# Second layer of a two-layer MoE: single-bank PSUM tiles, another emission order, some differences on GpSimd, two sums moved to the second phase

## The chip, the cores and the metric

The kernel runs on one core of one Trainium2 chip. The metric is device time in microseconds of one execution, as the median of several runs. The profile is of one more execution, and its times are counted from the start of that execution's span.

## The reference

Retention over 4 x 8 heads of 576 x 64 gives a matrix of 2304 tokens x 512. Two feed-forward layers follow, both with w_in of 512 x 2048 and w_out of 2048 x 512, all in float32:

```python
def _moe_ref(x, w_in, w_out):
    h = x @ w_in
    g = h * (1.0 / (1.0 + np.exp(-h)))
    return (g @ w_out).astype(np.float32)

def _moe2_ref(x, w_in, w_out):
    h = x @ w_in
    r = np.maximum(h, 0.0)
    g = r * r
    return (g @ w_out).astype(np.float32)

x = _moe_ref(x, moe_w_in, moe_w_out)
return _moe2_ref(x, moe2_w_in, moe2_w_out)
```

## The kernel before

Every float32 operand of a matmul is split in two: a high part, which ScalarE makes with a cast (L649), and a low part, the difference of value and high part, which VectorE makes (L650). A product of two operands takes three matmuls: high by high, high by low, low by high. `split` issues the cast at once and hangs the difference into `later`, a list that `flush` empties once per step.

Retention and the first layer fill the span up to 477 us. The second layer, which the change touches, is written by hand in two phases. Both use a scheme with seven products of half-size operands in place of eight (as Strassen's, in the form with few sums): operands 0 to 6 on each side are quarters of a matrix or sums of them, called a11, a12, a21, a22 and s1 (a21 + a22), s2 (s1 - a11), s3 (a11 - a21), s4 (a12 - s2). The weights' seven operands lie in DRAM ready made. Product i takes weight class RF[i], with RF = (0, 3, 1, 4, 2, 5, 6).

**Phase one** (`product1`, L719) makes h: three blocks b of tokens, four pairs d of weight columns p = 2d and 2d + 1 in each, and 14 steps k in a pair, k // 2 being the product i and k % 2 the column. A product is six matmuls of 128x384; there are 168 of them. `after1` reads the results from PSUM: a copy s1 by ScalarE after product 0 (L727), sums u2 and u3 of bank and copy by VectorE after products 1 and 3 (L731), then a quarter of h, c, after product 2 (ScalarE, relu, L735) and products 4, 5 and 6 (VectorE, L737). `gate1` turns c into g with relu and square on ScalarE (L748, L749); when the odd column's g is there, the tile is stored to gD in DRAM. S1 and S3 of g are made here, by two VectorE operations per pair (L756), and stored beside the quarters a11, a12 and a22: five tiles a pair.

**Phase two** (`product2`, L811) makes the output: nine sets P of 128 rows of each half, seven products of 24 matmuls of 128x256 in each. `after2` reads them in the same way (L819, L824, L826, L829) and issues the output's DMAs from ScalarE's queue. For set P, five tiles of g are loaded with SP's queue (`load_g`), two sums are made (`sum_g`) and seven operands split (`split_g`); the w2 classes are loaded (`load_w2`, L700, SP) and split (`split_w2`) in the last block of phase one (table in `beside1`) and in set 0 (the lists at the end). g's split for product n stands five products ahead.

One chain is the products 0 to 6 of one column or set. It has two PSUM banks; product i writes bank i % 2, and products 2, 3, 5 and 6 add to what is there. Which tile the chain gets is decided in `chain(n)`: every fourth one gets a single tile "pab" of two banks, the others two tiles of one bank each, "pa" and "pb". The dependencies are kept by tile.

What sets the order is the program's text: each engine's queue runs in the order of emission. In a step of phase one the product comes first, then `beside1` (loads, sums and splits of what comes later), then `flush`, then `after1`. The pool wp has 32 slots for weights, operands on load and g of set 0.

## Time and profile before

| | us |
|---|---|
| three runs | 874.85, 877.52, 878.30 |
| median | 877.52 |
| the profiled execution | 882.85 |
| its span in the trace | 881.0 |

| engine | busy us | share of the span |
|---|---|---|
| TensorE | 834.9 | 95% |
| VectorE | 511.9 | 58% |
| ScalarE | 452.5 | 51% |
| GpSimd | 103.0 | 12% |

The rows that the argument rests on stand in a section of their own below. PE is TensorE, DVE VectorE, ACT ScalarE, POOL GpSimd; SPq and ACTq are the DMAs that SP and ScalarE issue. A row of the timeline gives start, length, engine, line, operation, output<-input, and in brackets how long the engine had been idle before and what released it. GpSimd is idle after 477 us in this kernel.

### The profile page before, as it was taken

How to read it: one execution, taken by the hardware profiler on the slowest of the kernel's cores; microseconds unless marked ns; L12 is line 12 of the kernel's file. 1: busy time of each engine (PE TensorE's matmuls, PEld its weight loads, DVE VectorE, ACT ScalarE, POOL GpSimd, SP SyncE). 2: the span in 40 equal slices, each digit the busy share in tenths (PEclk: the TensorE clock that was granted, in tenths of full speed). 3: DMA queues.
4: the chain of work that ended last, by engine and by line, in shares of the span. 5: the costliest groups of instructions: out<-in, count | busy, mean ns of one | idle time of the engine just before them, and what ended most of it. 6: DMA issues, size and time to landing. Idle time of an engine off the chain costs nothing.

```text
span 881.0 us, 16063 instructions
## 1 busy us (share of the span) xinstructions
PE 834.9 (95%) x6458; PEld 769.1 (87%) x6458; DVE 511.9 (58%) x773; ACT 452.5 (51%) x874; POOL 103.0 (12%) x134
## 2 busy tenths in 40 slices
PE   6899989999999999999999998998997799989997
PEld 5778879999999888888887997998996799989996
DVE  4799984543544344423474777466567676655660
ACT  5687773453545334324464775565676443424430
POOL 3202001322232132201130000000000000000000
PEclk8999999999999999999999998998998999999999
DMA  9565642734546245217625654363597754444200
GB/s 347 176 182 192 216 145 73 227 138 141 172 139 203 108 139 164 89 42 230 200 78 209 215 197 139 108 214 108 193 320 242 282 192 168 157 132 156 97 25 25
DMA packets 70010, 144.96 MB, mean 165 GB/s; under 512 B 5552, under 2 KB 41392, under 8 KB 69936
## 3 DMA queue, kind: packets, MB, share of 16 engines
q1 hardware_dynamic: 63888, 132.66, 45.2%
q10 hardware_dynamic: 6048, 11.27, 3.4%
q8 instruction: 50, 0.82, 0.4%
q14 instruction: 24, 0.20, 0.1%
HBM read 96.21 MB, written 47.71 MB: 163 GB/s over the span
## 4 chain that ended last, share of the span: by engine, by line
PE 71%; ACT 5%; DVE 5%; DMA 4%; issue 2%; ACTq 0%; SPq 0%; DVEq 0%
PE acc L81 18%; PE ph L81 18%; PE pa L811 8%; PE pab L811 6%; PE pb L811 6%; PE pa L719 4%; PE pab L719 4%; PE pb L719 3%; PE Q L390 2%; DMA w2r<-w2c 2%; DMA gD<-g 1%; ACT xa L649 1%; ACT g L749 1%; PE P L339 1%; DMA gr<-gD 1%
## 5 line engine op out<-in xcount | busy, mean ns | idle before, releaser
L604 DVE TENSOR_TENSOR gl<-sg,gh 128x512 fp32r<-128x512 f32 (+1 forms) x80 | 54.6, 682 | 123.8 <-ACT gh L603 123.7
L81 PE MATMUL ph<-xh,wh 128*128 128x512 f32 (+2 forms) x328 | 121.1, 369 | 1.8 <-ACT xh L420 1.8
L601 ACT ACTIVATE sg<-ph 128x512 f32<-128x512 f32 (+1 forms) x80 | 44.2, 552 | 152.6 <-PE ph L81 151.5
L81 PE MATMUL acc<-gh,wh 128*128 128x512 f32 (+1 forms) x320 | 120.0, 375 | 0.0
L81 PE MATMUL ph<-xl,wh 128*128 128x512 f32 (+2 forms) x328 | 119.7, 365 | 0.3 <-DVE xl L422 0.3
L81 PE MATMUL ph<-xh,wl 128*128 128x512 f32 (+2 forms) x328 | 119.6, 365 | 0.0
L81 PE MATMUL acc<-gh,wl 128*128 128x512 f32 (+1 forms) x320 | 118.1, 369 | 0.0
L81 PE MATMUL acc<-gl,wh 128*128 128x512 f32 (+1 forms) x320 | 118.1, 369 | 0.0
L649 ACT CAST gl<-gr 128x1024 fp32r<-128x1024 f32 (+1 forms) x66 | 66.0, 1009 | 82.5 <-DVE y L829 34.8
L650 DVE TENSOR_TENSOR gl<-gr,gl 128x1024 fp32r<-128x1024 f32 (+1 forms) x66 | 77.0, 1174 | 49.9 <-ACT gl L649 49.9
L811 PE MATMUL pab<-w2s,gl 128*128 128x256 f32 x504 | 68.7, 295 | 17.0 <-ACT s L819 6.6
L811 PEld LDWEIGHTS pab<-w2s,gl 128*128 128x128 f32 x504 | 64.9, 201 | 20.6 <-ACT s L819 7.2
L719 PE MATMUL pa<-xa,w1s 128*128 128x384 f32 x432 | 81.9, 335 | 0.3 <-DVE c L737 0.3
L719 PEld LDWEIGHTS pa<-xa,w1s 128*128 128x128 f32 x432 | 75.4, 188 | 0.7 <-DVE c L737 0.6
L811 PE MATMUL pa<-w2s,gl 128*128 128x256 f32 x576 | 72.4, 283 | 0.0
L81 PEld LDWEIGHTS ph<-xh,wh 128*128 128x128 f32 x328 | 61.8, 188 | 10.2 <-ACT xh L420 2.3
L811 PEld LDWEIGHTS pa<-w2s,gl 128*128 128x128 f32 x576 | 70.6, 192 | 0.0
L81 PEld LDWEIGHTS ph<-xl,wh 128*128 128x128 f32 x328 | 61.8, 189 | 7.6 <-DVE xl L422 0.5
L81 PEld LDWEIGHTS ph<-xh,wl 128*128 128x128 f32 x328 | 61.7, 188 | 7.2
L81 PEld LDWEIGHTS acc<-gh,wh 128*128 128x128 f32 x320 | 60.4, 189 | 8.6
L81 PEld LDWEIGHTS acc<-gh,wl 128*128 128x128 f32 x320 | 60.4, 189 | 7.7
L81 PEld LDWEIGHTS acc<-gl,wh 128*128 128x128 f32 x320 | 60.5, 189 | 7.4
(112 smaller groups left out, 1353.9 us busy)
## 6 DMA issues: line engine op xcount, KB each, us to landing
wr<-w SPq DMA_DIRECT2D x64, 512.0 KB, 3.7
gD<-g SPq DMA_DIRECT2D x60, 384.0 KB, 2.9
gr<-gD SPq DMA_DIRECT2D x45, 512.0 KB, 5.1
raw<-att SPq DMA_DIRECT2D x32, 512.0 KB, 4.4
w2r<-w2c SPq DMA_DIRECT2D x14, 512.0 KB, 5.8
xq<-x SPq DMA_DIRECT2D x12, 384.0 KB, 5.4
out<-y ACTq DMA_DIRECT2D x18, 256.0 KB, 2.5
w1c<-wt SPq DMA_DIRECT2D x8, 512.0 KB, 7.9
```

Source lines behind the costliest of these rows:

```text
L81: mm(o, a, b, start=first and i == 0, stop=last and i == n - 1)
L339: mm(o, dims(u, a, e, b, 768), dims(u, a, e, b, 0), start=True, stop=True)
L390: mm(w, a, b, start=e not in started, stop=last)
L601: nc.scalar.activation(s, ph, ACTF.Silu)
L604: later.append(lambda: nc.vector.tensor_sub(gl, s, gh))
L649: nc.scalar.copy(dst[0], src)
L650: later.append(lambda: nc.vector.tensor_sub(dst[1], src, dst[0]))
L719: mm(o, lhs, rhs, start=m == 0 and i in (0, 1, 4), stop=m == 5, skip_group_check=True)
L749: later.append(lambda: nc.scalar.activation(g[:, :, p % 2], c.rearrange("p (t n) -> p t n", t=TT), ACTF.Square))
L811: mm(o, lhs, rhs, start=first, stop=m == NP - 1 and q == 2, skip_group_check=True)
```

## The change

- The PSUM tiles of the second layer come from one pool "pc" of eight tiles of one bank. Every chain takes two of them, in both phases; "pab" is gone. The first layer's PSUM pools are closed before.
- In both phases the reads of product n - 1 are emitted right behind product n and ahead of the loads, sums and splits of step n.
- i = 6 of the gate: one VectorE operation (scalar_tensor_tensor, max with 0, then times c) in place of relu and square on ScalarE.
- S1 and S3 of g are no longer made in phase one; four quarters are stored (48 stores instead of 60), four loaded per set (36 loads instead of 45), and S1 and S3 are made in phase two on VectorE as two more parts of `sum_g`, of 128x1024.
- The low part is made on GpSimd in 38 places: the x operands of blocks 1 and 2 other than operands 0 and 2 (ten of 128x768), the classes with odd c of the w1 columns from the third on (six of 128x512, six of 128x256), all those w2 splits that are called from `beside1` (classes 0, 3, 1 and two quarters of 4, 14 of 128x512), and operand 1 of set 0 (two of 128x512).
- In the last block the loads and splits of w2 and of set 0's g stand at other steps. In phase two the w2 splits start with the third quarter of class 4, and each set's loads and sums have other steps. The pool gq has 6 buffers instead of 7; the pools hl, rq and tq are opened in another order.

The core of the diff:

```diff
...
-    def chain(n):
-        if n % 4 == 0:
-            t = ps_a.tile([128, 2, 512], F32, tag="a", name="pab")
-            return t[:, 0], t[:, 1]
-        pool, tag = (ps_g, "g") if n % 4 == 1 else (ps_o, "o")
-        return tuple(pool.tile([128, 512], F32, tag=tag, name=nm) for nm in ("pa", "pb"))
-
-    def split(dst, src):
+    def chain():
+        return tuple(pools["pc"].tile([128, 512], F32, tag="c", name=nm) for nm in ("pa", "pb"))
+
+    def split(dst, src, engine=nc.vector):
...
-        later.append(lambda: nc.vector.tensor_sub(dst[1], src, dst[0]))
+        later.append(lambda: engine.tensor_sub(dst[1], src, dst[0]))
...
     def split_x(b, i, pool, tag):
...
-        split((t[:, 0], t[:, 1]), x_s[b][i])
+        split((t[:, 0], t[:, 1]), x_s[b][i], nc.gpsimd if b and i not in (0, 2) else nc.vector)
...
-    def split_w2(c, q):
+    def split_w2(c, q, engine=nc.vector):
...
-        split((t[:, 0], t[:, 1]), w2_raw[c, q // 2][:, q % 2 * 512 : q % 2 * 512 + 512])
+        split((t[:, 0], t[:, 1]), w2_raw[c, q // 2][:, q % 2 * 512 : q % 2 * 512 + 512], engine)
...
     def product1(p, b, i):
...
-            sp[p % 2] = {"o": chain(b * NP + p)}
+            sp[p % 2] = {"o": chain()}
...
-        if i != 2:
-            nc.scalar.activation(c, c, ACTF.Relu)
-        later.append(lambda: nc.scalar.activation(g[:, :, p % 2], c.rearrange("p (t n) -> p t n", t=TT), ACTF.Square))
+        to = g[:, :, p % 2]
+        c = c.rearrange("p (t n) -> p t n", t=TT)
+        if i == 6:
+            nc.vector.scalar_tensor_tensor(to, c, 0.0, c, op0=ALU.max, op1=ALU.mult)
+        else:
+            if i != 2:
+                nc.scalar.activation(c, c, ACTF.Relu)
+            later.append(lambda: nc.scalar.activation(to, c, ACTF.Square))
...
-            d = p // 2
-            now = [(2, 0, g)] if i == 2 else [(4, 2, g)] if i == 4 else [(6, 1, g)] if i == 6 else []
-            if i == 5:
-                a11, a22 = gt[2], gt[4]
-                s1 = pools["gq"].tile([128, TT, 2, 128], F32, tag="g", name="g")
-                later.append(lambda: later.append(lambda: (nc.vector.tensor_add(s1, g, a22), nc.vector.tensor_sub(g, a11, g))))
-                now = [(5, 3, s1), (5, 4, g)]
-
-            def store():
-                for _, q, t in now:
-                    to = gD[b, :, :, q, 2 * d : 2 * d + 2, :].rearrange("t p m n -> p t m n")
-                    nc.sync.dma_start(out=to, in_=t)
-
-            wait(3 if i == 5 else 2, store)
+            q, m = {2: 0, 6: 1, 5: 2, 4: 3}[i], p - 1
+            dst = gD[b, :, :, q, m : m + 2, :].rearrange("t p m n -> p t m n")
+            wait(2, lambda: nc.sync.dma_start(out=dst, in_=g))
...
-        if q == 4:
-            a11, a12, a22, s1, s3 = (g_raw[P, i] for i in range(5))
-            g_s[P] = [a11, a11, a12, s3, s1, a22, a12]
...
     def sum_g(P, part):
...
-        a11, a12, s1 = g_raw[P, 0], g_raw[P, 1], g_raw[P, 3]
+        a11, a12, a21, a22 = (g_raw.get((P, q)) for q in range(4))
...
-            nc.vector.tensor_sub(a11, s1, a11)
+            s1 = wp.tile([128, 1024], F32, tag="w", name="gs1")
+            nc.vector.tensor_add(s1, a21, a22)
+            g_s[P] = [a11, a11, a12, a21, s1, a22, a12]
+        elif part == 1:
+            nc.vector.tensor_sub(a21, a11, a21)
+        elif part == 2:
+            nc.vector.tensor_sub(a11, g_s[P][4], a11)
         else:
...
-    def split_g(P, i, pool):
+    def split_g(P, i, pool, engine=nc.vector):
...
-                split((t[:, 0], t[:, 1]), src[:, 512 * e : 512 * e + 512])
+                split((t[:, 0], t[:, 1]), src[:, 512 * e : 512 * e + 512], engine)
         else:
...
     def product2(P, i):
...
-            sp["2"] = {"o": chain(P)}
-        o = sp["2"]["o"][i % 2][:, 0:256]
+            sp["y", P % 2] = {"o": chain()}
+        o = sp["y", P % 2]["o"][i % 2][:, 0:256]
...
     def after2(P, i):
-        st = sp["2"]
+        st = sp["y", P % 2]
...
-                (2, 0): lambda: load_g(0, 0, "w", "w"),
-                (2, 2): lambda: load_g(0, 3, "w", "w"),
...
+                (1, 2): lambda: (load_g(0, 2, "w", "w"), load_g(0, 3, "w", "w")),
+                (1, 5): lambda: (load_g(0, 0, "w", "w"), load_g(0, 1, "w", "w")),
...
+                (2, 11): lambda: split_g(0, 1, "w", nc.gpsimd),
...
-                    split_w2(c, at.index((d, k)))
+                    split_w2(c, at.index((d, k)), nc.gpsimd)
...
+    ps_ctx.close()
+    pools["pc"] = ctx.enter_context(
+        tc.tile_pool(name="pc", bufs=8, space=bass.MemoryType.PSUM, reuse_waits="tile")
+    )
...
-    for name, bufs in (("gq", 7), ("cq", 1), ("tp", 1)):
+    for name, bufs in (("gq", 6), ("cq", 1), ("tp", 1)):
...
-    for b in range(NB2):
-        for d in range(NP // 2):
-            for k in range(14):
-                i, p = k // 2, 2 * d + k % 2
-                product1(p, b, i)
-                beside1(b, d, k)
-                flush()
-                after1(p, b, i)
-                if b == d == 0 and k == 1:
-                    split_x(0, 6, xp, x_home[6][1])
-                if b + 1 < NB2 and d == NP // 2 - 1 and k in (2, 6):
-                    sum_x(b + 1, 2 + k // 6)
-                if d == NP // 2 - 1 and k % 2 and b + 1 < NB2:
-                    pool, tag = x_home[i]
-                    split_x(b + 1, i, pools[pool], tag)
+    def behind1(b, d, k):
+        i, p = k // 2, 2 * d + k % 2
+        after1(p, b, i)
+        if b == d == 0 and k == 1:
+            split_x(0, 6, xp, x_home[6][1])
+        if b + 1 < NB2 and d == NP // 2 - 1:
+            if k % 2:
+                pool, tag = x_home[i]
+                split_x(b + 1, i, pools[pool], tag)
+            if k in (2, 6):
+                sum_x(b + 1, 2 + k // 6)
+
+    steps = [(b, d, k) for b in range(NB2) for d in range(NP // 2) for k in range(14)]
+    for n, (b, d, k) in enumerate(steps):
+        product1(2 * d + k % 2, b, k // 2)
+        if n:
+            behind1(*steps[n - 1])
+        beside1(b, d, k)
+        flush()
+    behind1(*steps[-1])
...
-    for name, bufs in (("tq", 1), ("rq", 6), ("hl", 6)):
+    for name, bufs in (("hl", 6), ("rq", 6), ("tq", 1)):
...
-            if n < 10:
-                at = (None, None, None, 0, 1, 3, 4, 5, 6, 6)[n]
+            if n < 14:
+                at = (None, None, None, 0, 1, 3, 4, 5, 6, 6, 7, 7, 8, 8)[n]
...
-                    do(at, lambda P=P, i=i: sum_g(P, i // 2), behind)
+                    do(at, lambda P=P, i=i: sum_g(P, 2 + i // 2), behind)
...
-            loads = (0, 0, 1, 1, 1) if P == 1 else (7 * P - 8, 7 * P - 8, 7 * P - 7, 7 * P - 7, 7 * P - 6)
-            for n, (q, pool, tag) in zip(loads, ((0, "rq", "r"), (3, "w", "w"), (1, "rq", "r"), (2, "rq", "r"), (4, "w", "w"))):
-                do(n, lambda P=P, q=q, pool=pool, tag=tag: load_g(P, q, pool, tag))
-    todo = [(4, q) for q in range(1, 4)] + [(c, q) for c in (2, 5, 6) for q in range(4)]
-    for (c, q), n in zip(todo, (0, 0, 0, 1, 1, 1, 2, 2, 2, 2, 3, 4, 4, 4, 5)):
+            n = 7 * P - 5
+            for q, at in ((2, n - 4), (3, n - 4), (0, n - 3), (1, n - 3)):
+                pool, tag = ("w", "w") if q == 2 else ("rq", "r")
+                do(max(at, 0 if q > 1 else 1), lambda P=P, q=q, pool=pool, tag=tag: load_g(P, q, pool, tag))
+            for part in range(2):
+                do(n - 1 + part + (2 if P == 1 else 0), lambda P=P, part=part: sum_g(P, part))
+    todo = [(4, q) for q in range(2, 4)] + [(c, q) for c in (2, 5, 6) for q in range(4)]
+    for (c, q), n in zip(todo, (0, 0, 1, 1, 1, 2, 2, 2, 3, 3, 4, 4, 5, 5)):
...
     for n in range(7 * NPP):
...
+        if n:
+            after2(*divmod(n - 1, 7))
...
-        after2(*divmod(n, 7))
...
+    after2(*divmod(7 * NPP - 1, 7))
...
```

What moves on three queues (rows of before, then of after):

TensorE's queue where block 1 begins; xa are x's operands, w1s the weights, pab, pa and pb the PSUM tiles with their numbers. Before:

```order
L719 MATMUL pab_5705<-xa_5566,w1s_4861 128x384 x6
L719 MATMUL pa_5719<-xa_5566,w1s_4874 128x384 x6
L719 MATMUL pab_5705<-xa_5589,w1s_4872 128x384 [waits Activation_49]
L719 MATMUL pab_5705<-xa_5589,w1s_4872 128x384 x5
L719 MATMUL pb_5720<-xa_5589,w1s_4908 128x384 x6
L719 MATMUL pab_5705<-xa_5609,w1s_4861 128x384 [waits DVE_49]
```

After:

```order
L716 MATMUL pa_5690<-xa_5564,w1s_4861 128x384 x6
L716 MATMUL pa_5704<-xa_5564,w1s_4874 128x384 x6
L716 MATMUL pb_5691<-xa_5585,w1s_4872 128x384
L716 MATMUL pb_5691<-xa_5585,w1s_4872 128x384 [waits Pool_49]
L716 MATMUL pb_5691<-xa_5585,w1s_4872 128x384 x4
L716 MATMUL pb_5705<-xa_5585,w1s_4908 128x384 x6
L716 MATMUL pa_5690<-xa_5605,w1s_4861 128x384 [waits Activation_49]
```

Before, the second product of the first column carried a wait for ScalarE, the third one a wait for VectorE. Now the second has none for ScalarE, only one for GpSimd at its second matmul, which reads a low part, and the third has the wait for ScalarE.

ScalarE's queue at the start of phase two; L819 and L826 (before), L813 and L820 (after) are the reads of products 0 and 2 of set 0, w2s the weights, gl the operands of g. Before:

```order
L649 CAST gl<-gr 128x1024
L649 CAST w2s<-w2r 128x512 x3
L819 COPY s_7024<-pab 128x256
L649 CAST gl<-gr 128x1024
L649 CAST w2s<-w2r 128x512 x7
L826 COPY y<-pab 128x256
```

After:

```order
L646 CAST gl<-gr 128x1024
L646 CAST w2s<-w2r 128x512 x2
L813 COPY s_6990<-pa 128x256
L646 CAST gl<-gs_6555 128x1024
L646 CAST w2s<-w2r 128x512 x6
L820 COPY y<-pa 128x256
```

Two casts of weights less stand ahead of the read of product 2, those ahead of it being the four of class 2 and the first two of class 5 in the new order.

VectorE's queue from set 0's fifth product (L829, L823) to the read of set 1's second (L824, L818); gr are loaded quarters, L786, L788, L780 and L782 sums in place, L775 and L778 S1 and S3. Before:

```order
L829 TENSOR_TENSOR y<-pab,u_7147 128x256
L650 TENSOR_TENSOR gl<-gr,gl 128x1024 x2
L650 TENSOR_TENSOR w2s<-w2r,w2s 128x512
L829 TENSOR_TENSOR y<-pab,s_7024 128x256
L786 TENSOR_TENSOR gr<-gr 128x1024
L650 TENSOR_TENSOR gl<-gr,gl 128x1024 x3
L829 TENSOR_TENSOR y<-pab,u_7074 128x256
L788 TENSOR_TENSOR gr<-gr 128x1024
L650 TENSOR_TENSOR gl<-gr,gl 128x1024 x2
L824 TENSOR_TENSOR u_7328<-pb,s_7295 128x256
```

After:

```order
L823 TENSOR_TENSOR y<-pa,u_7113 128x256
L647 TENSOR_TENSOR gl<-gr,gl 128x1024
L647 TENSOR_TENSOR w2s<-w2r,w2s 128x512 x2
L780 TENSOR_TENSOR gr<-gs_7078,gr 128x1024
L823 TENSOR_TENSOR y<-pb,s_6990 128x256
L647 TENSOR_TENSOR gl<-gr,gl 128x1024 x2
L782 TENSOR_TENSOR gr<-gr 128x1024
L823 TENSOR_TENSOR y<-pa,u_7038 128x256
L647 TENSOR_TENSOR gl<-gr,gl 128x1024
L647 TENSOR_TENSOR gl<-gs_7078,gl 128x1024
L775 TENSOR_TENSOR gs_7267<-gr 128x1024
L647 TENSOR_TENSOR gl<-gr,gl 128x1024 x2
```

Set 2's S1 (gs_7267) has come in ahead of the read of set 1's second product, and a low part of weights stands later than it did.

## Rows read from the trace of the kernel before

**Rows 1.** TensorE's waits in phase one: us in total, times, longest us

```profile
PE pab L719 <- ACT s L727: 7.5, 3, 3.5
PE pa L719 <- DVE c L737: 0.3, 1, 0.3
```

**Rows 2.** Matmuls of line 719 into pab: ns min/median/max, first and last start

```profile
L719 PE MATMUL pab<-xa,w1s x252: 331/335/688, 477.2 to 654.5; 128*128 128x384 f32 x126
```

**Rows 3.** Chain of work that ended last: start us, us to the next

```profile
500.65 2.09 PE pb L719 x12
...
715.64 2.88 PE pb L811 x24
...
767.49 2.89 PE pab L811 x24
...
792.15 2.88 PE pa L811 x24
...
874.25 3.14 PE pab L811 x24
```

**Rows 4.** TensorE's timeline at the starts of blocks 1 and 2

```profile
540.68 1.21 PE L719 MATMUL pa<-xa,w1s 128*128 128x384 f32 x6
545.42 2.29 PE L719 MATMUL pab<-xa,w1s 128*128 128x384 f32 x6 [3.53 <-ACT s L727]
...
551.04 1.20 PE L719 MATMUL pa<-xa,w1s 128*128 128x384 f32 x6
...
605.46 1.21 PE L719 MATMUL pa<-xa,w1s 128*128 128x384 f32 x6
...
615.85 1.20 PE L719 MATMUL pa<-xa,w1s 128*128 128x384 f32 x6
```

**Rows 5.** TensorE's timeline at the start of phase two

```profile
670.96 3.03 PE L811 MATMUL pab<-w2s,gl 128*128 128x256 f32 x24
679.67 4.94 PE L811 MATMUL pab<-w2s,gl 128*128 128x256 f32 x24 [5.68 <-ACT s L819]
...
692.80 3.13 PE L811 MATMUL pab<-w2s,gl 128*128 128x256 f32 x24 [1.62 <-ACT y L826]
...
706.84 3.04 PE L811 MATMUL pa<-w2s,gl 128*128 128x256 f32 x24
```

**Rows 6.** ScalarE's timeline at the boundary and at the start of phase two

```profile
544.91 0.46 ACT L727 COPY s<-pab 128x384 f32<-128x384 f32 x1
...
683.47 1.14 ACT L649 CAST w2s<-w2r 128x512 fp32r<-128x512 f32 x2 [2.91 <-DMA w2r<-w2c]
...
690.57 1.91 ACT L649 CAST w2s<-w2r 128x512 fp32r<-128x512 f32 x3 [4.62 <-DMA w2r<-w2c]
```

**Rows 7.** SP's DMA issues at the start of phase two

```profile
674.99 1.77 SPq L776 DMA_DIRECT2D gr<-gD  x2
676.86 0.89 SPq L700 DMA_DIRECT2D w2r<-w2c  x2
```

**Rows 8.** VectorE by line and form, 477 us on: busy us, mean ns; idle before

```profile
L650 DVE TENSOR_TENSOR gl<-gr,gl 128x1024 fp32r<-128x1024 f32 x60 | 73.1, 1223 | 49.9 <-ACT gl L649 49.9
L756 DVE TENSOR_TENSOR g<-g 128x768 f32<-128x768 f32 x24 | 22.9, 954 | 0.4
...
L650 DVE TENSOR_TENSOR w2s<-w2r,w2s 128x512 fp32r<-128x512 f32 x28 | 18.7, 687 | 11.0 <-ACT w2s L649 10.9
L650 DVE TENSOR_TENSOR xa<-xq,xa 128x768 fp32r<-128x768 f32 x13 | 12.4, 956 | 5.2 <-ACT xa L649 4.7 <-PE pb L719 0.5
...
L829 DVE TENSOR_TENSOR y<-pa,u 128x256 f32<-128x256 f32 x12 | 5.1, 421 | 3.2 <-PE pa L811 3.2
```

**Rows 9.** GpSimd's two-input operation, and one case beside VectorE

```profile
L192 POOL TENSOR_TENSOR wt<-t x16: 727/735/1451, 154.2 to 460.0; 128x256 f32<-128x256 f32 x16
...
440.63 1.32 POOL L189 TENSOR_TENSOR wt<-t,wt 128x256 f32<-128x256 f32 x1 [4.11 <-DVE t L116]
...
441.39 1.38 DVE L670 TENSOR_TENSOR xq<-xs,xq 128x768 f32<-128x768 f32 x1
```

More of the change, by code (lines that the diff above doesn't have):

```diff
@@ L622, in gemm2 @@
                 nc.scalar.dma_start(out=x2[:, t, tok0[j] : tok0[j] + n], in_=y)
-    gD = dp.tile([NB2, TT, 128, 5, NP, 128], F32, name="gD")
+    gD = dp.tile([NB2, TT, 128, 4, NP, 128], F32, name="gD")
     x_raw = {}
@@ L690, in split_w1 @@
         src = w1_raw[p, c // 2][:, c % 2 * 512 : c % 2 * 512 + n]
-        split((t[:, 0, c0 : c0 + n], t[:, 1, c0 : c0 + n]), src)
+        split((t[:, 0, c0 : c0 + n], t[:, 1, c0 : c0 + n]), src, nc.gpsimd if p > 1 and c % 2 else nc.vector)
     def w1_at(p, c):
@@ L851, in beside1 @@
                 (1, 0): lambda: (load_w2(0, 0), load_w2(0, 1)),
-                (1, 10): lambda: load_w2(3, 0),
+                (1, 2): lambda: (load_g(0, 2, "w", "w"), load_g(0, 3, "w", "w")),
+                (1, 5): lambda: (load_g(0, 0, "w", "w"), load_g(0, 1, "w", "w")),
+                (1, 12): lambda: (load_w2(3, 0), sum_g(0, 0)),
                 (1, 13): lambda: load_w2(3, 1),
-                (2, 0): lambda: load_g(0, 0, "w", "w"),
-                (2, 2): lambda: load_g(0, 3, "w", "w"),
-                (2, 4): lambda: (load_w2(1, 0), load_g(0, 1, "w", "w")),
-                (2, 7): lambda: load_w2(1, 1),
-                (2, 9): lambda: load_g(0, 2, "w", "w"),
-                (2, 11): lambda: load_g(0, 4, "w", "w"),
-                (3, 1): lambda: split_g(0, 0, "w"),
-                (3, 3): lambda: sum_g(0, 0),
-                (3, 5): lambda: (split_g(0, 1, "w"), load_w2(4, 0)),
-                (3, 8): lambda: load_w2(4, 1),
-                (3, 9): lambda: split_g(0, 2, "w"),
-                (3, 11): lambda: sum_g(0, 1),
-            }
-            for c, at in ((0, ((1, 4), (1, 6), (1, 9), (1, 11))), (3, ((2, 1), (2, 2), (2, 5), (2, 6))), (1, ((3, 0), (3, 2), (3, 3), (3, 4))), (4, ((3, 12),))):
+                (2, 0): lambda: sum_g(0, 1),
+                (2, 1): lambda: split_g(0, 0, "w"),
+                (2, 3): lambda: sum_g(0, 2),
+                (2, 8): lambda: load_w2(1, 0),
+                (2, 11): lambda: split_g(0, 1, "w", nc.gpsimd),
+                (2, 12): lambda: load_w2(1, 1),
+                (3, 6): lambda: load_w2(4, 0),
+                (3, 7): lambda: (split_g(0, 2, "w"), load_w2(4, 1)),
+                (3, 9): lambda: sum_g(0, 3),
+            }
+            for c, at in (
[4 rows of a table added]
+            ):
                 if (d, k) in at:
-                    split_w2(c, at.index((d, k)))
+                    split_w2(c, at.index((d, k)), nc.gpsimd)
             if (d, k) in todo:
```

7 lines of the change are left out of this document (4 added, 3 removed), and 4 rows, old and new, of the table todo.

## The prediction, on record before the changed kernel ran

> **What bounds the kernel now.** I read the chain of work that ended last first. In the second layer it is almost one unbroken row of TensorE groups [rows 3], so the question is where TensorE waits. Its own pace comes from the same rows: in phase one a group of 12 matmuls, two products, takes 2.09 us, so a product takes 1.045 us; in phase two a product of 24 matmuls starts 2.88 us after the one before. Phase one begins at 477.2 us [rows 2], and phase two at 670.96 us [rows 5].
>
> *Phase one.* 168 products at 1.045 us are 175.6 us; 670.96 − 477.2 is 193.8. So **18.2 us are lost**. Most of the waits are for reads of the two-bank tile "pab" [rows 1], which every fourth chain uses: product i+1 has to wait there until product i's bank has been read, though it writes the other bank. At the start of block 1 this is to be seen singly [rows 4]: a column's product 0 into pab, the other column's into pa from 540.68, then 3.53 us of nothing until ScalarE's copy of pab, which starts only at 544.91 behind casts and gates of the block before [rows 6]; then six matmuls take 2.29 us instead of 1.20, which I read as the clock having dropped while TensorE idled. From 540.68 to 551.04 four products take 10.36 us where 4 × 1.045 are 4.18: 6.2 lost. Block 2's start shows the same pattern, 605.46 to 615.85 [rows 4] (10.39 us), so the two boundaries cost 12.4 and the other pab waits the remaining 5.8.
>
> *Phase two.* 63 products at 2.88 us are 181.4 us; from 670.96 to 877.39, the end of the last group [rows 3], are 206.4. So **25.0 us are lost**, and set by set from the starts in [rows 3, 5]: set 0, 670.96 to 706.84, 35.88 where 7 × 2.88 are 20.16: 15.7. Set 4, 767.49 to 792.15: 4.5. Sets 5 to 8, 792.15 to 877.39, 85.24 where 80.64 are due: 4.6, and since set 8 is the next pab chain, it is its. Sets 1 to 3 lose 0.2. Sets 0, 4 and 8 are exactly those with a pab tile; but set 0 loses over three times as much as set 4, by waits of 5.68 and 1.62 us [rows 5] that come from elsewhere, weights that land late (below).
>
> **The change, part by part.** All sums are made against the profiled execution (882.85 us, of which 881.0 are the span). It is 5.33 above the median of 877.52; I take the same difference off the median.
>
> *Single banks in phase one.* Every chain gets two tiles of one bank, so the waits of product 1 for the read of product 0, of 2 for 1 and so on go. What is left is the wait for the read two steps further back: product 2 waits for the copy of product 0, as the other three quarters of the chains do now with 0.3 us lost in all on pa [rows 1]. At a boundary that copy is late by 3.53 us now; it is asked for two products, 2.09 us, later, so 1.4 would stay if ScalarE were as late as it is. It will be earlier: relu and square of the last product's gate go from ScalarE to one VectorE operation, which takes from ScalarE two relus and two squares in each pair of columns, each at least as long as its copy of this shape, 0.46 us [rows 6], so 1.8 us. I take 0.75 us left per boundary, **1.5 in all; term 1 is −16.7**. Bounds: nothing left (−18.2), or the 1.4 stays at both and the clock drops again, about 1.6 each (six and six matmuls at up to 1.09 us more than 1.20): −12.2.
>
> *VectorE in phase one.* Leave: the 24 sums of line 756, 0.954 each, 1.9 us per pair; 10 low parts of the x operands at 0.956, so 4.8 us in each pair ahead of a boundary [rows 8]. Come: 24 fused gates of 128x384, half the elements of line 756's, so about 0.5 each and 1.0 us per pair. VectorE's queue gets shorter where TensorE waited for it. I count nothing for that beyond term 1.
>
> *Sets 4 and 8.* Only the pab waits are there to lose: 4.5 + 4.6, **term 2 is −9.1**. S1 and S3 of a set come in as two more sums of 1.22 us, so VectorE's work per set goes from 7 low parts, 2 sums and 5 reads, 9 × 1.22 + 5 × 0.42 = 13.1 us, to 15.5 of the 20.16 that TensorE needs [rows 8]. It stays hidden; if it came to late reads at set edges, some 3 us over eight sets, which is my bound (−6).
>
> *The start of phase two.* Here removing pab does not remove the loss, since weight class 5, for product 4, isn't there. Now its cast starts at 690.57, which is 19.6 us after the phase starts, when its load lands [rows 6]. SP issues two loads of w2 at 676.86 [rows 7], and ScalarE waits for the first of them until 683.47; class 5's come later in the same queue, behind three loads of the next set's g. In the new order product 4 waits for ScalarE's copy of product 2's bank, which still stands behind the casts of class 5's first load; products 3, 5 and 6 wait for VectorE reads that stand behind the low parts; and set 1's product 3 waits for the read of its product 1, behind nearly all of VectorE's work of the start: 14 × 1.22 + 8 × 0.69 + 5 × 0.42 = 24.7 us [rows 8]. Before, from that cast (690.57) to set 1's product 3 (715.64, [rows 3]) are 25.1 us, so this chain decides in both kernels, and its start is what can move. The last stores of g, which the loads wait for on SP, come about 2.2 us sooner (line 756's step is gone from between gate and store), and one load of g fewer stands ahead of class 5's. Eight loads go from SP between 674.99 and the landing at 690.57, 15.6/8 = 1.95 us each. So the landing goes from 19.6 to 19.6 − 2.2 − 1.95 = 15.4 us after the start; bounds 11.6 (issued 5 us after the start, a little ahead of class 2's 5.9 now, and landing in that load's 6.6 us) and 19.6 (no change). Set 1's product 3 then starts at 15.4 + 25 = 40.4, where ten products would be done at 28.8: 11.6 lost, against 15.9 by the same account before. I book **−4.1, term 3**, with bounds of −7.9 and +2.5; the latter is no earlier landing and ScalarE's queue held by the outputs' DMA issues, which now stand ahead of the next casts and wait for VectorE's sums (two of them, 1.22 us each).
>
> *GpSimd.* It gets 38 differences: 22 of 128x512, 6 of 128x256, 10 of 128x768. The trace has its two-input operation at 128x256 alone, 0.735 us in the middle [rows 9]; by multiples 1.47 and 2.2, an upper bound if there is a fixed part. 22 × 1.47 + 6 × 0.74 + 10 × 2.2 = 58.8 us over phase one's 194. GpSimd is idle there now, and most low parts are read by TensorE many products after their cast, so I count 0. If that cover is gone, the price is a VectorE operation that runs beside one of them: at 440.63 both were longer, GpSimd's 1.32 instead of 0.735 and VectorE's L670 1.38 instead of 0.95, a rise of 0.43 to 0.59 [rows 9].
>
> The Trainium skill has a rule that speaks against this part: "SBUF — State Buffer", section "Who interferes with whom", says that a VectorE instruction with two SBUF inputs and a GpSimd instruction that reads SBUF exclude each other, the later one standing for the whole of the other. The rows at 440 agree with it. By it the sum would grow by whatever of the 58.8 us falls on VectorE at a moment when TensorE waits for VectorE; by the row's rise it is at most 38 × 0.59 = 22 us of VectorE's time, of which VectorE's idle time takes nearly all.
>
> *Stores and loads.* 48 stores of g for 60 and 36 loads for 45: less traffic; counted in term 3 where SP's queue is on the path, at 0 elsewhere (sets 1 to 3 lose 0.2 now, so there is nothing to gain).
>
> **Sum**: −16.7 − 9.1 − 4.1 = −29.9. Profiled 882.85 − 29.9 = 853.0; of the median 877.52, **847.6 us**.
>
> **The rivals.**
>
> *The start of phase two comes no sooner* (chance 0.14). For it: the landing is set by DMA, of which the trace shows only waits, and more loads are drawn together at that point. Against it: fewer stores and loads. Sets 0 and 1 lose 15.8 to 18 as now or more: 850 to 856.
>
> *GpSimd gets on the path in part* (0.13). In phase one's blocks 1 and 2 and in phase two's start, VectorE's sums of bank and copy have one SBUF input and the low parts two; if a low part on VectorE is held each time, the reads queued behind it are late. A sixth of the 58.8 us on the path is +10: 857, range 853 to 862.
>
> *The change doesn't do what it says* (0.06): single banks, but the reads are as late as before, so product 2 waits where product 1 did, and only about 40% of terms 1 and 2 come. 877.5 − 0.4 × 30: 865.
>
> *Slower* (0.03). The mechanism is that of the second rival with all of its price: each GpSimd difference holds VectorE for its whole length, and TensorE with it, from block 1 to the end of set 0. All 58.8 give 877.5 − 29.9 + 58.8 = 906; it decides from 29.9/58.8 = 51% on. Against it: VectorE is not the engine TensorE waits for in most steps, and 0.3 us is lost on the single-bank tiles now.
>
> **How the numbers follow.** Forecast 0.62 (840 to 853, the bounds of terms 1 and 3), the rivals 0.14, 0.13, 0.06 and 0.03, and 0.02 for below 840. The range, 840 to 861, leaves out the last two rivals, part of the second and what is below. A measurement of this kernel tells some 0.5%, 4.4 us, from no change. Faster by more: all but the slow rival and some of the third, 0.94; within: 0.03; slower: 0.03.
>
> **What would show it.** Phase one should last about 177 us, with the two starts of blocks 1 and 2 at 2.09 us per pair of products and the granted clock unbroken; a wait of over 1 us there for ScalarE's copy means that term 1 is too large. Sets 4 and 8 should take 20.2 us each. The start of phase two should still show one wait for weights, with class 5's cast some 15 us in; sets 0 and 1 together should lose 11 to 12 us. GpSimd's differences of 128x512 should take 1.5 us or less; many of twice that length, with VectorE's low parts at more than 1.22 or 0.69, and TensorE's waits put down to GpSimd or to VectorE's reads, would be the lock. The prediction is wrong if phase one loses over 6 us, if any set from 2 on loses more than 1 us, or if the start loses more than it does now.

## The result and the profile after

The changed kernel takes **851.2 us** (849.6 to 852.5) where the kernel before takes 877.6: a ratio of 0.970, 95% interval [0.968, 0.973]. The forecast was 847.6, the range 840 to 861. The profiled execution of the changed kernel takes 851.46 us, its span 849.7.

First the three stretches of the second layer: phase one, the first twenty or so products of phase two, the rest. Columns: stretch, length, busy us and instructions of TensorE, its weight loads, VectorE, ScalarE and GpSimd, granted clock of TensorE, share of the DMA engines, GB/s.

```profile
475.70:650.70 175.00, 175.00 (x1010) 174.84 (x1009) 108.02 (x176) 112.27 (x227) 53.75 (x38) 1.00 0.53 178
650.70:710.80 60.10, 50.98 (x387) 49.54 (x387) 44.90 (x54) 27.80 (x39) 0.61 (x1) 0.94 0.61 210
710.80:846.20 135.40, 135.36 (x1128) 135.15 (x1127) 90.72 (x101) 48.33 (x55) 0.00 (x0) 1.00 0.30 95
```

TensorE is busy in every microsecond of phase one, at full clock, with VectorE at 108 us and ScalarE at 112 of 175. From 710.8 on it idles no more either. All that is left stands in the 60 us in between. The waits of TensorE there (us in total, times, longest):

```profile
PE pb L805 <- DVE u L818: 5.8, 4, 4.7
PE pa L805 <- ACT s L813: 2.5, 1, 2.5
PE pa L805 <- DVE y L823: 0.7, 1, 0.7
```

By the prediction's own account (168 products at 1.045 us, 63 at 2.88): phase one lost 18.2 us and now −0.6, 193.8 to 175.0; phase two lost 25.0 and now 14.1, 206.4 to 195.5. Together that is −29.7 us; the spans differ by 31.3, because phase one starts 1.5 us earlier in this execution, after a first layer whose instructions are the same.

The start of phase two on TensorE, which answers to [rows 5]:

```profile
650.69 3.03 PE L805 MATMUL pa<-w2s,gl 128*128 128x256 f32 x24
...
664.14 4.57 PE L805 MATMUL pb<-w2s,gl 128*128 128x256 f32 x24 [4.66 <-DVE u L818]
...
687.85 4.63 PE L805 MATMUL pa<-w2s,gl 128*128 128x256 f32 x24 [2.51 <-ACT s L813]
692.77 3.14 PE L805 MATMUL pb<-w2s,gl 128*128 128x256 f32 x24 [0.28 <-DVE u L818]
```

ScalarE there, answering to [rows 6]; ACTq is its DMA issue:

```profile
661.16 2.38 ACT L646 CAST w2s<-w2r 128x512 fp32r<-128x512 f32 x4 [3.86 <-DMA w2r<-w2c]
666.29 1.14 ACT L646 CAST w2s<-w2r 128x512 fp32r<-128x512 f32 x2 [2.75 <-DMA w2r<-w2c]
...
679.69 0.34 ACTq L826 DMA_DIRECT2D out<-y  x1
680.08 2.00 ACT L646 CAST gl<-gr 128x1024 fp32r<-128x1024 f32 x2 [3.91 <-DVE y L823]
685.15 0.34 ACTq L826 DMA_DIRECT2D out<-y  x1
685.54 1.04 ACT L646 CAST gl<-gr 128x1024 fp32r<-128x1024 f32 x1 [3.46 <-PE pb L805]
...
687.43 0.36 ACT L813 COPY s<-pa 128x256 f32<-128x256 f32 x1
```

VectorE:

```profile
661.81 1.94 DVE L647 TENSOR_TENSOR w2s<-w2r,w2s 128x512 fp32r<-128x512 f32 x3 [3.25 <-ACT w2s L646]
663.67 0.42 DVE L818 TENSOR_TENSOR u<-pb,s 128x256 f32<-128x256 f32 x1
...
681.16 2.36 DVE L647 TENSOR_TENSOR gl<-gr,gl 128x1024 fp32r<-128x1024 f32 x2 [1.50 <-ACT gl L646]
683.56 1.23 DVE L782 TENSOR_TENSOR gr<-gr 128x1024 f32<-128x1024 f32 x1
684.70 0.42 DVE L823 TENSOR_TENSOR y<-pa,u 128x256 f32<-128x256 f32 x1
```

Two stories are to be read. First, class 2 lands at 661.16, 10.5 us into the phase; VectorE's read of product 1's bank (663.67) stands behind three of class 2's low parts, though product 3, which waits for it, needs class 4. Second, ScalarE's issue of the first output at 679.69 waits for a sum y on VectorE; the two casts behind it wait with it; VectorE makes their low parts from 681.16 on, then a sum, and only then the next y at 684.70; the next issue, two more casts, and the copy at 687.43 that set 1's product 2 waits for. After either stall the granted clock is 0.50, the lower level of 1.2 GHz:

```profile
664.14:666.30 2.16, 2.16 (x10) 2.16 (x11) 0.54 (x1) 0.01 (x1) 0.00 (x0) 0.50 1.01 404
687.85:690.20 2.35, 2.35 (x11) 2.35 (x12) 2.35 (x3) 2.35 (x3) 0.00 (x0) 0.50 0.51 99
```

so that 24 matmuls take 4.57 and 4.63 us instead of 3.04, 1.5 more each.

### The profile page after: what moved, and what is told of

It reads as the page before. It is cut to its first block, busy times and chain, and to the rows that moved or that the text cites. A ratio compares the mean times of both kernels' runs of the same rounds, so it can differ in the third digit from the quotient of the medians.

```text
span 849.7 us, 16010 instructions
## 1 busy us (share of the span) xinstructions
PE 825.0 (97%) x6458; PEld 764.2 (90%) x6458; DVE 503.8 (59%) x753; ACT 431.4 (51%) x826; POOL 158.1 (19%) x172
## 4 chain that ended last, share of the span: by engine, by line
PE 79%; DVE 3%; DMA 2%; ACT 1%; issue 1%; SPq 0%; ACTq 0%; DVEq 0%
PE acc L82 19%; PE ph L82 19%; PE pa L716 12%; PE pa L805 10%; PE pb L716 9%; PE pb L805 8%; PE Q L391 2%; DVE gl L647 1%; DMA w2r<-w2c 1%; PE P L340 1%; PE P L345 1%; DVE w2s L647 1%; DMA raw<-att 0%; ACT gl L646 0%; DVE gr L780 0%
## 5 line engine op out<-in xcount | busy, mean ns | idle before, releaser
L805 PE MATMUL pa<-w2s,gl 128*128 128x256 f32 x864 | 110.0, 286 | 3.2 <-ACT s L813 2.5
L805 PEld LDWEIGHTS pa<-w2s,gl 128*128 128x128 f32 x864 | 107.2, 194 | 3.7 <-ACT s L813 2.7
L716 PE MATMUL pa<-xa,w1s 128*128 128x384 f32 x576 | 105.9, 335 | 0.0
L716 PEld LDWEIGHTS pa<-xa,w1s 128*128 128x128 f32 x576 | 100.4, 188 | 0.1
L805 PE MATMUL pb<-w2s,gl 128*128 128x256 f32 x648 | 84.2, 287 | 5.9 <-DVE u L818 5.8
L805 PEld LDWEIGHTS pb<-w2s,gl 128*128 128x128 f32 x648 | 81.1, 195 | 6.9 <-DVE u L818 5.8
L646 ACT CAST gl<-gr 128x1024 fp32r<-128x1024 f32 (+1 forms) x57 | 56.5, 1004 | 56.1 <-DVE y L823 19.0
L716 PE MATMUL pb<-xa,w1s 128*128 128x384 f32 x432 | 80.9, 335 | 0.0
L647 DVE TENSOR_TENSOR gl<-gr,gl 128x1024 fp32r<-128x1024 f32 (+1 forms) x55 | 64.7, 1183 | 24.6 <-ACT gl L646 24.3
L716 PEld LDWEIGHTS pb<-xa,w1s 128*128 128x128 f32 x432 | 75.4, 188 | 0.1
```

The lines of the kernel that those rows point to most:

```text
L646: nc.scalar.copy(dst[0], src)
L647: later.append(lambda: engine.tensor_sub(dst[1], src, dst[0]))
L716: mm(o, lhs, rhs, start=m == 0 and i in (0, 1, 4), stop=m == 5, skip_group_check=True)
L805: mm(o, lhs, rhs, start=first, stop=m == NP - 1 and q == 2, skip_group_check=True)
```

## The experiments

Each kernel was compared with the kernel before on the same chip. These chips are not the same for all rows, so two kernels are best compared by their ratios. "Lost" is by the account above, from the one profiled execution of each kernel; those of e2_pab, e5_oldsums and e12_nopool were 2.3 to 2.8 us above their medians, that of e6_reads 2.6 below.

| kernel | median us | ratio to before, 95% | phase one lost | phase two lost |
|---|---|---|---|---|
| before | 877.6 | 1 | 18.2 | 25.0 |
| changed | 851.2 | 0.970 [0.968, 0.973] | −0.6 | 14.1 |
| e1_banks | 855.7 | 0.974 [0.973, 0.976] | 4.3 | 12.8 |
| e2_pab | 865.5 | 0.986 [0.984, 0.988] | 6.0 | 23.4 |
| e3_vector | 851.8 | 0.970 [0.968, 0.973] | 0.7 | 15.5 |
| e4_gate | 854.4 | 0.973 [0.971, 0.976] | 1.4 | 15.4 |
| e5_oldsums | 857.7 | 0.976 [0.974, 0.978] | 7.9 | 13.5 |
| e12_nopool | 855.7 | 0.975 [0.973, 0.977] | 5.7 | 13.5 |
| e6_reads | 850.6 | 0.968 [0.966, 0.970] | −0.5 | 13.2 |
| e7_early | 847.4 | 0.964 [0.963, 0.966] | −0.6 | 11.5 |
| e9_pool | 850.7 | 0.969 [0.967, 0.970] | −0.6 | 14.3 |
| e10_out | 849.1 | 0.967 [0.965, 0.969] | −0.5 | 12.6 |
| e11_mix | 844.4 | 0.963 [0.960, 0.966] | −0.5 | 9.3 |
| e13_best | 841.9 | 0.960 [0.957, 0.962] | −0.6 | 6.1 |

**The banks alone (e1_banks).** On the kernel before:

```diff
     def chain(n):
-        if n % 4 == 0:
...
+        return tuple(pools["pc"].tile([128, 512], F32, tag="c", name=nm) for nm in ("pa", "pb"))
```

> The kernel before with one part of the change alone: all chains of the second layer take two single-bank tiles from one pool of eight; gate, sums, low parts, loads and their order stay. Theory (the waits belong to the two-bank tile, nothing else of the change is needed for them): phase one loses 1.5 to 6 us of 193.8 instead of 18.2 (at the two boundaries product 2 may still wait 1.4 us each for ScalarE's copy), sets 4 and 8 lose under 1 us each instead of 4.5, set 0 loses as before some 15 us; 877.6 - 14 - 9 = 854, between 850 and 859. Rival (the reads come late because ScalarE and VectorE are too full, and the rest of the change empties them): the waits move to product 2, more than half of the loss stays, 864 or more.

22 of the 26 us come with this edit. TensorE's timeline of this kernel at the starts of blocks 1 and 2:

```profile
540.97 2.34 PE L716 MATMUL pa<-xa,w1s 128*128 128x384 f32 x12 [1.43 <-ACT s L724]
600.99 2.37 PE L716 MATMUL pa<-xa,w1s 128*128 128x384 f32 x12 [1.45 <-ACT s L724]
```

The 3.53 us of [rows 4] have become 1.43 and 1.45, which is 3.53 less two products, and 12 matmuls behind them take 2.34 us. The granted clock is 1.00 there; in the kernel before, behind the 3.53 us, it was 0.50:

```profile
545.42:547.50 2.08, 2.08 (x6) 2.08 (x7) 0.66 (x1) 0.74 (x2) 0.00 (x0) 0.50 1.02 341
```

The start of phase two loses 12.8 instead of the 15.9 of the prediction's account (25.0 less 9.1 for sets 4 and 8); it needs no other part of the change for that.

**The banks undone (e2_pab).** On the changed kernel:

```diff
+        if n % 4 == 0:
+            t = pools["pab"].tile([128, 2, 512], F32, tag="a", name="pab")
+            return t[:, 0], t[:, 1]
```

> The changed kernel with the banks alone undone: every fourth chain has a two-bank tile again, beside six single-bank ones. Theory (banks): the pab waits return, 9 us in sets 4 and 8 and, with ScalarE lighter than before, 8 to 18 us in phase one: 851 + 17 to 27 = 868 to 878. Rival (lighter queues make the reads early enough): under 860.

865.5, under the 868 expected, and above the rival's 860. Phase two loses 9.3 more than the changed kernel. For sets 4 and 8 9.1 were priced; the trace has 3.8 and 3.9 there, 1.2 in set 5 and 0.5 in the start. In these two sets products 0 and 1 now run without a break (48 matmuls in 5.92 us), since the new order emits the read of product 0 behind product 1. Phase one loses only 6.6 more. The boundaries show why:

```profile
540.13 1.31 PE L719 MATMUL pab<-xa,w1s 128*128 128x384 f32 x6 [1.79 <-ACT s L727]
600.35 1.32 PE L719 MATMUL pab<-xa,w1s 128*128 128x384 f32 x6 [1.30 <-ACT s L727]
```

With the rest of the change in place the same wait is 1.79 and 1.30 instead of 3.53, and six matmuls after it take 1.31 instead of 2.29: the granted clock is 1.00. So banks and relief are partly two ways to the same gain. How much of the relief is the gate's, and how much that of the moved sums and GpSimd, this run does not tell.

**GpSimd (e3_vector).** All 38 low parts on VectorE; one of the four places:

```diff
-        split((t[:, 0], t[:, 1]), x_s[b][i], nc.gpsimd if b and i not in (0, 2) else nc.vector)
+        split((t[:, 0], t[:, 1]), x_s[b][i], nc.vector)
```

> The changed kernel with all 38 low parts on VectorE, none on GpSimd. Theory (these parts are hidden on either engine, since VectorE is busy under two thirds of phase one): 851 within 2 us. Rival 1 (VectorE's relief is needed at the block boundaries and where w2 is split): 3 to 10 us slower, with TensorE waiting for VectorE's low parts or reads in phase one. Rival 2 (GpSimd holds VectorE through the shared access to SBUF, and that reaches TensorE): 2 us or more faster, the start of phase two above all.

No difference: 0.970 and 0.970. VectorE's work does change, though: it is busy 108 us of phase one with GpSimd's help and 124 without. By form, the changed kernel on GpSimd, then the same two groups of VectorE in the changed kernel and in this one, all in phase one (busy us, mean ns):

```profile
L647 POOL TENSOR_TENSOR w2s<-w2r,w2s 128x512 fp32r<-128x512 f32 x14 | 19.2, 1388 | 29.8 <-ACT w2s L646 25.6 <-PE pa L716 2.3 <-PE pb L716 1.8
L647 POOL TENSOR_TENSOR xa<-xq,xa 128x768 fp32r<-128x768 f32 x8 | 15.7, 1967 | 63.6 <-ACT xa L646 62.2 <-DVE g L747 1.4
```

```profile
L747 DVE SCALAR_TENSOR_TENSOR g<-c 128x384 f32<-128x384 f32 x23 | 15.4, 668 | 0.8
L647 DVE TENSOR_TENSOR w1s<-w1r,w1s 128x512 fp32r<-128x512 f32 x12 | 11.2, 938 | 2.9 <-ACT w1s L646 2.8
```

```profile
L647 DVE TENSOR_TENSOR w1s<-w1r,w1s 128x512 fp32r<-128x512 f32 x18 | 12.3, 687 | 4.2 <-ACT w1s L646 4.2
L747 DVE SCALAR_TENSOR_TENSOR g<-c 128x384 f32<-128x384 f32 x22 | 12.3, 557 | 0.7
```

VectorE's operations with two SBUF inputs are longer on the mean while GpSimd works, 938 against 687 and 668 against 557 ns; its reads of banks are not (555 against 553). So in these two groups alone VectorE pays back 12 × 0.25 + 23 × 0.11 = 5.5 us of what GpSimd takes off it. It didn't reach TensorE.

**The gate (e4_gate).**

```diff
-        if i == 6:
-            nc.vector.scalar_tensor_tensor(to, c, 0.0, c, op0=ALU.max, op1=ALU.mult)
...
+        if i != 2:
+            nc.scalar.activation(c, c, ACTF.Relu)
+        later.append(lambda: nc.scalar.activation(to, c, ACTF.Square))
```

> The changed kernel with the gate of product 6 back on ScalarE as relu and square (48 operations more there, 24 fewer on VectorE). Theory of the prediction (ScalarE's relief removes the rest of the boundary wait): phase one loses 1.4 us more at each of two boundaries, up to 3 us with the clock: 852 to 857. Rival (the copy of product 0 has two products of slack and is early anyway): 851 within 1 us; it could be faster by a little, since VectorE's fused gates stand at the start of phase two ahead of its low parts.

The waits that the prediction's step speaks of are there, but smaller than the 1.4 each that was expected:

```profile
537.87 2.34 PE L716 MATMUL pa<-xa,w1s 128*128 128x384 f32 x12 [0.95 <-ACT s L724]
596.89 2.36 PE L716 MATMUL pa<-xa,w1s 128*128 128x384 f32 x12 [0.46 <-ACT s L724]
```

Phase one is 2.0 us longer than in the changed kernel, the median 3.2.

**The sums left in phase one (e5_oldsums, then e12_nopool).** e5_oldsums has the banks, GpSimd's low parts and the fused gate. It keeps S1 and S3 in phase one, the old tables and also the old emission order, which its recorded text does not say. Against the changed kernel, `gate1` ends as in the kernel before:

```diff
-            q, m = {2: 0, 6: 1, 5: 2, 4: 3}[i], p - 1
...
+                later.append(lambda: later.append(lambda: (nc.vector.tensor_add(s1, g, a22), nc.vector.tensor_sub(g, a11, g))))
+                now = [(5, 3, s1), (5, 4, g)]
```

e12_nopool is the same with the low parts on VectorE, as in e3_vector.

> All of the change but the move of S1 and S3 of g and the new tables of the last block and of phase two: banks, GpSimd's low parts and the fused gate on the kernel before; S1 and S3 are made and stored in phase one as before. Theory (the banks and ScalarE's relief make phase one whole, and the sums' move changes only the start of phase two): phase one loses under 1 us, sets 2 to 8 nothing, and the start some 12 to 14 us as in the kernel with the banks alone (12.8) and the changed one (14.1): 849 to 853. Rival (the move of the sums and the new tables are what shortened the start): the start loses 15 to 17, 853 to 857.

> The kernel of e5_oldsums (banks, fused gate, S1 and S3 in phase one, old tables) with its 36 low parts back on VectorE. Theory (in that kernel phase one lost 7.9 us since GpSimd's low parts made VectorE's two-input operations longer, 128x512 at 1.05 us instead of 0.685, with reads of the banks queued behind): phase one loses under 3 us, 852 to 855. Rival (the fused gate overfills VectorE as long as the sums stay in phase one, and GpSimd only helps it): phase one loses 8 us or more, 857 to 862.

My theory fell twice. Phase one loses 7.9 us where under 1 was expected, so the moved sums are not a matter of phase two alone. And GpSimd is not the cause either: without it 5.7 are still lost, and the ratios, 0.976 and 0.975, have overlapping intervals. e12_nopool on TensorE, and VectorE ahead of the first of these waits:

```profile
544.33 2.36 PE L716 MATMUL pb<-xa,w1s 128*128 128x384 f32 x12 [1.33 <-DVE u L728]
604.53 2.36 PE L716 MATMUL pb<-xa,w1s 128*128 128x384 f32 x12 [1.33 <-DVE u L728]
```

```profile
540.53 1.94 DVE L757 TENSOR_TENSOR g<-g 128x768 f32<-128x768 f32 x2
...
543.73 1.01 DVE L728 TENSOR_TENSOR u<-pb,s 128x384 f32<-128x384 f32 x2
```

At the boundaries the wait for ScalarE has become one for VectorE's read, and L757, the two sums, stands ahead of that read with 1.94 us. In e3_vector, which has no GpSimd either but the sums moved, VectorE's queue at this place is the same without these two, and TensorE does not wait there. The fused gate moves the load from the one engine to the other, and only where the sums leave VectorE too does the boundary come out clean: phase one loses 4.3 with neither (e1_banks), 5.7 with the gate alone (e12_nopool), 1.4 with the sums moved alone (e4_gate, which has GpSimd's low parts besides), 0.7 or less with both. The first two can't be told apart by time (ratios 0.974 and 0.975); what differs is the engine that is waited for. The emission order is no rival in phase one: the two loops give every engine's queue the same order there. What the old tables of the last block add in e5_oldsums and e12_nopool was not tried apart from the sums; they do not touch the two boundaries.

**The start of phase two, one edit each.** Splits of classes 2 and 5 a step later (e6_reads):

```diff
-    for (c, q), n in zip(todo, (0, 0, 1, 1, 1, 2, 2, 2, 3, 3, 4, 4, 5, 5)):
+    for (c, q), n in zip(todo, (0, 0, 2, 2, 2, 2, 3, 3, 3, 3, 4, 4, 5, 5)):
```

> The changed kernel with the splits of w2 classes 2 and 5 one step later in phase two, so that VectorE's read of set 0's product 1 stands ahead of class 2's low parts and ScalarE's copy of product 2 ahead of class 5's casts. Theory (at the start the reads of the banks stand behind splits of weights that wait for their landing): the wait of 4.66 us ahead of product 3 goes, product 4 then waits for class 2 itself and product 5 for class 5; 2 to 5 us faster, 846 to 849. Rival (VectorE has too much work in sets 0 and 1, wherever it stands): the waits move behind, 851 within 1 us.

Class 2 loaded ahead of the last stores (e7_early):

```diff
+                (3, 13): lambda: (load_w2(2, 0), load_w2(2, 1)),
...
-    for n, c, e in ((0, 2, 0), (0, 2, 1), (1, 5, 0), (1, 5, 1), (2, 6, 0), (3, 6, 1)):
+    for n, c, e in ((1, 5, 0), (1, 5, 1), (2, 6, 0), (3, 6, 1)):
```

> The changed kernel with the two loads of w2 class 2 issued in the last step of phase one, ahead of the last three stores of g, instead of behind them; all else stays. Theory (class 2 lands late because its issue stands on SP behind stores that wait for gates): class 2 is cast some 4 us sooner, product 3 starts some 4 us sooner, 2 to 5 us faster in all, 846 to 849. Rival (the landing isn't what decides, VectorE's queue is): 851 within 1 us.

Twelve more low parts on GpSimd (e9_pool):

```diff
-        do(n, lambda c=c, q=q: split_w2(c, q))
+        do(n, lambda c=c, q=q: split_w2(c, q, nc.vector if c == 4 else nc.gpsimd))
```

> The changed kernel with the low parts of w2 classes 2, 5 and 6 on GpSimd too (12 of 128x512, 1.39 us each there in the changed kernel, 0.685 on VectorE). Theory (VectorE's queue of some 33 us up to set 1's product 3 bounds sets 0 and 1): 8 us of work leave it, 3 to 6 us faster, 845 to 848. Rival 1 (the landing decides): under 1 us. Rival 2 (GpSimd holds VectorE's sums and low parts, which are denser here than in phase one): 851 to 855, with VectorE's 128x1024 at 1.5 us or more on the mean of the start.

Outputs issued a step later (e10_out):

```diff
-                nc.scalar.dma_start(out=out[r0 : r0 + 128, :], in_=st["y"][h])
+                wait(1, lambda: nc.scalar.dma_start(out=out[r0 : r0 + 128, :], in_=st["y"][h]))
```

> The changed kernel with the outputs' DMA issues in phase two one step later in ScalarE's queue, behind the casts of that step instead of ahead of them. Theory (the issue waits for VectorE's sum y, the casts behind it wait with it, VectorE then waits for these casts before it can make the next y: this hand-over holds set 1's product 2 by 2.5 us): that wait goes, and with it some slow clock; 2 to 4 us faster, 847 to 849. Rival (VectorE's queue of some 33 us is as long either way): 851 within 1 us.

How finely may phase two's column be read? The changed kernel, e3_vector and e4_gate have the same start but for ScalarE's and VectorE's last gates and two low parts, and lose 14.1, 15.5 and 15.4: a difference under 1.5 us says little.

Only e7_early clearly gains what was expected, 3.8 us by the medians. e6_reads and e9_pool change the median by half a us: in e6_reads the 4.66 us are gone and 3.32 and 1.52 stand at products 5 and 4; in e9_pool 5.08 stand at product 4 and the low parts on GpSimd themselves hold product 6 (2.4 us in three waits). e10_out, on TensorE:

```profile
684.96 3.04 PE L805 MATMUL pa<-w2s,gl 128*128 128x256 f32 x24
690.60 4.35 PE L805 MATMUL pb<-w2s,gl 128*128 128x256 f32 x24 [2.61 <-DVE u L818]
```

Set 1's product 2 waits no more; product 3 waits 2.61 us instead, for VectorE. 2.1 us of the median are left of the edit, 0.967 against 0.970 with overlapping intervals.

**All together (e11_mix), and without GpSimd (e13_best).** e11_mix has e6_reads, e7_early and e10_out, and the odd quarters of classes 2, 5 and 6 on GpSimd. e13_best keeps these on VectorE, splits classes 5 and 6 later still, and makes set 2's S1 and S3 behind the read of set 1's product 1. Against the changed kernel, without the lines of e7_early and e10_out that both have:

```diff
-    for (c, q), n in zip(todo, (0, 0, 1, 1, 1, 2, 2, 2, 3, 3, 4, 4, 5, 5)):
+    for (c, q), n in zip(todo, (0, 0, 2, 2, 2, 2, 4, 4, 4, 4, 5, 5, 5, 5)):
...
-                do(n - 1 + part + (2 if P == 1 else 0), lambda P=P, part=part: sum_g(P, part))
+                do(n - 1 + part + (2 if P == 1 else 1 - part if P == 2 else 0), lambda P=P, part=part: sum_g(P, part))
```

> The changed kernel with four edits at the start of phase two: class 2 loaded ahead of the last stores, classes 2 and 5 split one step later, the odd quarters of classes 2, 5 and 6 with their low part on GpSimd (six of 128x512, 4.1 us off VectorE), the outputs' issues one step later. Theory (three queues hold the start one after the other: SP's for class 2, VectorE's for the reads, ScalarE's for set 1): the start loses 3 to 8 us of the 14.1, 840 to 845. Rival (VectorE's sums and low parts bound sets 0 and 1 whatever stands around them): no better than the early load alone, 846 to 849.

> The changed kernel with the start of phase two written in another order, all its low parts of w2 on VectorE: class 2 loaded ahead of the last stores; class 2 split two steps, class 5 four, class 6 five steps after the start, so that each read of a bank stands ahead of the splits that its next product doesn't need; the outputs' issues one step later; S1 and S3 of set 2 behind the read of set 1's product 1. Theory (the reads' place in VectorE's and ScalarE's queues is what the start loses, and GpSimd's parts in e11_mix cost VectorE more than they took from it): the start loses 4 to 7 us instead of 9.3, 839 to 843. Rival (VectorE's sum of work up to set 1's product 3, some 33 us against 28.8, can't be ordered away): 8 to 10 us lost, 844 to 846.

e11_mix takes 844.4, within what was expected: 9.3 us stay lost, 4.8 fewer than in the changed kernel. VectorE in its start, by form from 655 to 672 us:

```profile
L647 DVE TENSOR_TENSOR w2s<-w2r,w2s 128x512 fp32r<-128x512 f32 x6 | 7.5, 1256 | 0.8 <-ACT w2s L646 0.8
L647 DVE TENSOR_TENSOR gl<-gr,gl 128x1024 fp32r<-128x1024 f32 x3 | 4.7, 1572 | 0.0
L778 DVE TENSOR_TENSOR gr<-gr 128x1024 f32<-128x1024 f32 x1 | 2.0, 1965 | 0.0
```

Against 685, 1222 and 1217 ns alone these are 6 × 0.57 + 3 × 0.35 + 0.75 = 5.2 us more, where six low parts given away save 4.1. So e13_best gives none away; there the same two forms are back at 681 and 1215 ns. It is the fastest kernel here, **841.9 us**, 4% under the kernel before and, by the two ratios, 0.960 / 0.970, 1.1% under the changed one. Its interval overlaps that of e11_mix, and it has the later splits besides, so what leaving GpSimd out brings is not shown by itself. What is left on TensorE:

```profile
663.65 3.02 PE L808 MATMUL pb<-w2s,gl 128*128 128x256 f32 x23 [1.15 <-DVE w2s L647]
...
667.53 5.89 PE L808 MATMUL pa<-w2s,gl 128*128 128x256 f32 x47 [0.74 <-DVE w2s L647]
...
680.59 3.13 PE L808 MATMUL pb<-w2s,gl 128*128 128x256 f32 x24 [1.40 <-DVE u L821]
...
688.10 3.14 PE L808 MATMUL pb<-w2s,gl 128*128 128x256 f32 x24 [1.51 <-DVE u L821]
```

All four waits are for VectorE, and none is followed by half clock.

## Why the prediction was right, and where it was not

*Term 1, −16.7: −18.8 measured.* The mechanism was right. The copy asked for two products later leaves 1.43 and 1.45 us in e1_banks (1.4 was worked out). ScalarE's relief was worked out at 1.8 us; e2_pab, with everything but the banks, has 3.53 less 1.79, so 1.7, at block 1, though not by the gate alone. Both together take the wait away, and e4_gate, without the relief, has 0.95 and 0.46 of it back. The 0.75 us per boundary that I left standing were not needed; 0.6 us more is the pace, 175.0 / 168 = 1.042 instead of 1.045. What I counted at nothing, VectorE's relief by the moved sums, was a condition: e12_nopool shows the wait that would have stood there.

*Term 2, −9.1: right.* From 710.8 us on nothing is lost, with VectorE busy 91 of 135 us; e2_pab brings 8.9 back in sets 4, 5 and 8.

*Term 3, −4.1: 15.9 to 14.1, so −1.8, and less by the executions with 15.5.* The landing came as forecast: class 5's first cast came 15.6 us into the phase (666.29), 15.4 was forecast. The step that failed is "so this chain decides in both kernels, and its start is what can move". The 25.1 us that it was read from are no sign of a chain through VectorE. In the kernel before, the read of set 1's product 1 was done at 714.22, 1.3 us ahead of product 3, which did not wait; the 25.1 are TensorE's own pace with set 0's last waits for pab in it.

```profile
713.80 0.42 DVE L824 TENSOR_TENSOR u<-pb,s 128x256 f32<-128x256 f32 x1
```

```profile
715.48 3.04 PE L811 MATMUL pb<-w2s,gl 128*128 128x256 f32 x24
```

And where class 5 came later, set 1's product 3 did not. e1_banks, whose phase two begins at 655.91, has the cast 18.6 us into it and the product at 41.3:

```profile
674.47 1.14 ACT L646 CAST w2s<-w2r 128x512 fp32r<-128x512 f32 x2 [4.44 <-DMA w2r<-w2c]
```

```profile
697.24 3.04 PE L808 MATMUL pb<-w2s,gl 128*128 128x256 f32 x24
```

In e12_nopool these are 19.3 and 42.0, in the changed kernel 15.6 and 42.1 (692.77, 26.5 behind the cast, where 25 was forecast). So 3 us of earlier landing bought nothing that shows, and what fell from 15.9 came with the banks alone (12.8), of which the prediction said that removing pab does not remove the loss there. What held the changed kernel instead are the two stalls read above. ScalarE's output issues stand ahead of the casts, which I had named in the bound and not booked (without this, e10_out has the product at 39.6), and each of the two stalls was followed by the lower clock, 1.5 us more each time. One statement was plainly wrong besides: class 5 feeds product 5, not product 4 (RF says so); product 4 waits behind class 5's casts only by its place in ScalarE's queue. So I missed that the first stall, 4.66 us at product 3, is a read queued behind class 2's low parts, and that class 2's landing was the one to move: e7_early, 3.8 us.

*The sum.* The account's −29.7 meets the −29.9 of the forecast because term 1 gave 2.1 us more and term 3 2.3 less than was booked. That these cancel is luck.

*GpSimd at 0: right,* for the reason given. Its price was 54 us in all where 58.8 was the upper bound (1.39 us for 128x512, 1.97 for 128x768). The Trainium skill's rule ("SBUF — State Buffer", section "Who interferes with whom", the later of the two stands for the whole of the other) fits one case that the trace shows singly: the fused gate of 0.56 us that starts at 650.50, while GpSimd is in an operation until 651.31, ends at 651.73 (651.87 by the rule), and it has two SBUF inputs.

```profile
650.01 1.30 POOL L647 TENSOR_TENSOR w2s<-w2r,w2s 128x512 fp32r<-128x512 f32 x1 [1.27 <-ACT w2s L646]
```

```profile
650.50 1.23 DVE L747 SCALAR_TENSOR_TENSOR g<-c 128x384 f32<-128x384 f32 x1
```

The rival built on it did not come: phase one had VectorE time to spare, 67 us of 175. In the start of e11_mix, where VectorE was busy 16.2 of 17 us, GpSimd cost VectorE more time than it gave, 5.2 against 4.1.

*The median.* It fell by 26.4 us, the account by 29.7. The profiled execution of before was 5 us above its median, the one of after 0.3: taking the whole difference off the median was too much, and which stretch the 3 us belong to no trace here shows.
